# Value products moved behind the next pair's first score tiles, and the preparation of pairs moved further ahead

## The chip, the cores and the metric

The kernel runs on one core of a Trainium2 chip. The metric is the device time of one execution in microseconds, as the median of several runs. The core's engines run side by side, each through its own queue in order: TensorE (PE, with its weight loads PEld), VectorE (DVE), ScalarE (ACT), GpSimd (POOL) and SyncE (SP), whose queue issues all DMA transfers here.

## The reference

Sigmoid attention over 8 batches, 12 heads, 448 positions and 64 channels a head, followed by a feed-forward layer on 3584 tokens of width 768 with 2048 hidden units:

```python
scores = scale * np.matmul(q, k.transpose(0, 1, 3, 2)) - np.log(S)
attn = 1.0 / (1.0 + np.exp(-scores))
attn_out = np.matmul(attn, v)
x = attn_out.transpose(0, 2, 1, 3).reshape(B * S, H * D)
h = x @ w_in
g = np.where(h > 0.0, h, np.exp(np.minimum(h, 0.0)) - 1.0)
out = g @ w_out
```

Everything is float32 outside. Inside, after the first batch, each operand is split into a high and a low float16 part, and a product is made of three matmuls (high by high, low by high, high by low).

## The kernel before, in words

The work goes by batches `b` = 0 to 7 and, in a batch, by six pairs of heads `hp` = 0 to 5; `n = 6 b + hp` numbers the pairs. Batch 0 is computed in float32, while the two weight matrices are loaded, measured and split (`w_in_part`, `load_w_out`). From batch 1 on, TensorE, ScalarE, VectorE and SP keep the order in which the program is written (`manual_schedule`); GpSimd and all that comes earlier are ordered by a scheduler.

A pair is prepared in three steps, which `prepare_pair(n)` hands out one after the other. *Measure*: VectorE takes the largest magnitudes of the values (`mx<-rv`) and of queries and keys (`mt<-raw`), and spreads them on a diagonal (`dg`). *Scale* (`second`): TensorE sums the diagonal over the partitions (`pb`), VectorE reduces it (`al`, `pw`) and takes reciprocals, GpSimd makes the scales (`sc`). *Split* (`third`): ScalarE writes the high parts of queries, keys (`nat`) and values (`vn`), VectorE the low ones; SP issues the DMA that transposes `nat` into `qk`. The raw data lie in two buffers each (`raw`, and the two tiles `rvs` for values); the loads of a pair that comes two later follow the split in SP's queue, since that split empties their buffer.

A pair's own work is `scores(t)` for four tiles t (score tiles `psc` in PSUM, two buffers; the fourth tile is half as wide), `soften(t)` (sigmoid `sg` and scaled high part `at` on ScalarE, low part on VectorE), `values(t)` (value products, summed in `pav`), and `finish` (`xh`, the split result). At the end of a batch `hidden` rescales `xh` and calls `moe1`, which makes 16 tiles `ph` of 18 matmuls, whose exponentials and splits (`e`, `g`) ScalarE and VectorE do. The second product of the previous batch, `moe2`, is cut into steps of three matmuls each, 16 to a tile `po` of 48; `fill(n)` puts n such steps wherever TensorE would wait. An odd batch b has 96 steps (the product of an even batch has no tile of remaining rows), an even one 128. The PSUM tiles `po`, `pb` and most `ph` share three buffers (`pm`).

Before, a pair of a batch from 1 on runs on TensorE as: scores 0 and 1, five steps (eight in pair 0), scores 2 and 3, the rest of its share of steps, `pb`, its own four `values`. Between the first scores and the five steps the next pair is split and pair n + 3 is loaded; after the five steps pair n + 2 is measured, and behind the rest of the share it is scaled.

Of the kernel before, what the change touches and what calls it, by code (L numbers as in the profile page):

```python
# [9 lines left out]
F16 = mybir.dt.float16  # L10
BF16 = mybir.dt.bfloat16
F32 = mybir.dt.float32
# [20 lines left out]
def attention_ffn(  # L33
# [9 lines left out]
    nc = tc.nc  # L43
# [10 lines left out]
    HM = DM // NH  # L54
    SB, OB, AB = 4, 3, 3
    WF = 2
    WR, WT = 3, 2
    EXACT = 1
    SP = 4
    SKEW = 2  # L60
    W_IN = [1, 2, 3, 5, 6, 8, 8]
    W_LOAD = [1, 1]
# [236 lines left out]
    def prepare(b, hp, raw, rv, xs):  # L299
# [19 lines left out]
        def scales():  # L319
            product()  # L320
            sc = sb.tile([P, n + 3], F32, tag="sc", name=f"sc{u}", bufs=3)
            if b >= EXACT:
# [13 lines left out]
        def transposed(sc):  # L336
# [12 lines left out]
            for t, n_t, s in (  # L349
# [5 lines left out]
                )  # L355
            qk = sb.tile([P, 2, 2 * NC + 1, P], F16, tag="qk", name=f"qk{u}", bufs=2)
            nc.sync.dma_start_transpose(
# [3 lines left out]

            vn = sb.tile([P, 2, 2 * NC + 2, D], F16, tag="vn", name=f"vn{u}", bufs=2)
            split(vn[:, 0], vn[:, 1], rv, sc[:, 0:1])
# [4 lines left out]
    class Pair:  # L368


        def __init__(self, b, hp, x_scale, s_scale, qk, vs, xh, xs):
            self.b, self.hp, self.u = b, hp, f"{b}_{hp}"
            self.x_scale, self.s_scale = x_scale, s_scale
            self.qk, self.vs, self.xh, self.xs = qk, vs, xh, xs
            self.psc, self.sg, self.pav = {}, {}, None
# [46 lines left out]
        def values(self, g):  # L422
            if g == 0:
                self.pav = ps.tile([P, 512], F32, tag="pav", name=f"pav{self.u}")
            pav, sg, vv = self.pav, self.sg.pop(g), self.vs
            parts = [(0, 0), (1, 0), (0, 1)][: 2 * len(vv) - 1]
            for n, (i, k) in enumerate(parts):
                if g == NC:
                    nc.tensor.matmul(  # L429
                        pav[:, :S], vv[i][:, 2 * NC :].rearrange("p t d -> p (t d)"),  # L430
                        sg[k][:, 0], start=False, stop=(n == len(parts) - 1),
                    )
                    continue
                for j in range(2):
                    nc.tensor.matmul(  # L435
                        pav[rows[j], :S], vv[i][:, j * NC + g], sg[k][:, j],
                        start=(g == 0 and n == 0), stop=False,
                    )

        def finish(self):  # L440
            hp, xh = self.hp, self.xh
            split(xh[:, hp, 0], xh[:, hp, 1], self.pav[:, :S], self.x_scale)
            absmax(self.xs[:, 2, hp : hp + 1], xh[:, hp, 0])
# [37 lines left out]
    def moe1(b, g, xh, m, first, beside=None):  # L481
# [8 lines left out]
        for f in range(NF):  # L490

            if f == 3:
                ph = ps.tile([P, 512], F32, tag="pav", name=f"ph{b}_{f}")
            elif f == 8:
                ph = ps.tile([P, 2, 512], F32, tag="psc", name=f"ph{b}_{f}", bufs=2)[:, 0]
            else:
                ph = ps.tile([P, 512], F32, tag="pm", name=f"ph{b}_{f}", bufs=3)
# [100 lines left out]
    def prepare_pair(n):  # L598
# [4 lines left out]
        if hp == 0:  # L603
            xh_of[b] = sb.tile([P, NK, 2, S], F16, tag="xh", name=f"xh{b}", bufs=2)
            xs_of[b] = sb.tile([P, 3, NP], F32, tag="xs", name=f"xs{b}", bufs=2)
# [23 lines left out]
    def pair_of(n):  # L629
        b, hp = pairs[n]  # L630
        return Pair(b, hp, *ready.pop(n), xh_of[b], xs_of[b])

    def hidden(b, beside=None):

        xh, xs = xh_of.pop(b), xs_of.pop(b)
        whole = rescale(b, xh, xs)
# [24 lines left out]
    for n in range(EXACT * NP):  # L661
# [12 lines left out]
        for f in range(W_IN[n], W_IN[n + 1]):  # L674
            load_w_in(1)
            w_in_part(f)
    third = prepare_pair(EXACT * NP + 1)()
    load_pair(EXACT * NP + 2)
# [5 lines left out]


    E = mybir.EngineType
    with tc.manual_schedule(engines={E.PE, E.Activation, E.DVE, E.SP}):
        for b in range(EXACT, B):
# [4 lines left out]
            def fill(n):  # L693
                nonlocal left
                left -= n
                for _ in range(n):
                    next(tiles, None)

            for hp in range(NP):
                n = b * NP + hp  # L700
                share = left // (NP - hp)
                tail = 4 if hp == NP - 1 else 0
                p = pair_of(n)
                for t in range(2):
                    p.scores(t)
                    p.soften(t)
                third()
                if n + 3 < len(pairs):
                    loaded[n + 3] = load_qk(*pairs[n + 3]), load_v(*pairs[n + 3])

                gap = 8 if hp == 0 else 5
                fill(gap)
                second = prepare_pair(n + 2)
                for t in range(2, NC + 1):
                    p.scores(t)
                    p.soften(t)
                if b == EXACT and hp < NC:

                    step(3 if hp < NC - 1 else NF)
                if hp == NP - 1:  # L720
                    h = hidden(b)
                    next(h)
                fill(share - gap - tail)
                third = second()
                for t in range(NC + 1):
                    p.values(t)
                p.finish()
                fill(tail)
                if b == EXACT and hp == NC - 1:
                    out_scale(*of_moe2, slice(1, NH))  # L730
# [34 lines left out]
```

## Time and profile before

| | |
|---|---|
| median of 3 runs | 1274.88 us (1273.56 to 1275.74) |
| profiled execution | 1272.11 us, its span 1270.3 us |
| mean granted TensorE clock | 0.981 |
| TensorE busy | 1192.9 us, 94% of the span |
| VectorE busy | 841.5 us, 66% |
| ScalarE busy | 703.2 us, 55% |
| batch 0 and its weights, to the first output matmul | 170.83 us |
| attention of batch 1 | 100.66 us |
| attention of batches 2 / 3 / 7 | 96.42 / 87.70 / 84.88 us |
| first feed-forward product of a batch | 54.63 us |

"Attention of a batch" is the stretch from its first score tile (in batch 1, from the first output matmul) to the first matmul of `moe1`; it holds the steps of the previous batch's `moe2` as well. A row of the order-of-time view has start, length, engine, line, operation and tiles, and in brackets the idle time before it with what ended it. Where a length covers several instructions, the last one's tail is in it, so that durations are better read from start to start.

### The profile page before, as it was taken

How to read it: one execution, taken by the hardware profiler on the slowest of the kernel's cores; microseconds unless marked ns; L12 is line 12 of the kernel's file. 1: busy time of each engine (PE TensorE's matmuls, PEld its weight loads, DVE VectorE, ACT ScalarE, POOL GpSimd, SP SyncE). 2: the span in 40 equal slices, each digit the busy share in tenths (PEclk: the TensorE clock that was granted, in tenths of full speed). 3: DMA queues.
4: the chain of work that ended last, by engine and by line, in shares of the span. 5: the costliest groups of instructions: out<-in, count | busy, mean ns of one | idle time of the engine just before them, and what ended most of it. 6: DMA issues, size and time to landing. Idle time of an engine off the chain costs nothing.

```text
span 1270.3 us, 19231 instructions
## 1 busy us (share of the span) xinstructions
PE 1192.9 (94%) x7240; PEld 606.2 (48%) x7240; DVE 841.5 (66%) x1852; ACT 703.2 (55%) x1039; POOL 62.7 (5%) x269
## 2 busy tenths in 40 slices
PE   6779868999999998999999999999999999999998
PEld 2224434545455554445555554545455554455565
DVE  3787979875677657875677655885577756765500
ACT  5875878744666336754566436763566435673400
POOL 0000001000000000100000100000000000100000
PEclk8998989999999999999999999999999999999999
DMA  7836423420144203430144201440034401420000
GB/s 223 282 103 166 157 75 86 103 69 1 43 86 92 50 1 65 104 88 1 21 94 92 63 1 43 90 110 15 1 86 92 92 1 22 100 50 7 1 25 26
DMA packets 207133, 89.73 MB, mean 71 GB/s; under 512 B 177344, under 2 KB 196800, under 8 KB 207040
## 3 DMA queue, kind: packets, MB, share of 16 engines
q1 hardware_dynamic: 207040, 88.51, 28.1%
q8 instruction: 56, 0.92, 0.3%
q14 instruction: 37, 0.30, 0.1%
HBM read 58.20 MB, written 11.01 MB: 54 GB/s over the span
## 4 chain that ended last, share of the span: by engine, by line
PE 66%; DVE 12%; ACT 11%; DMA 5%; issue 5%; SPq 1%; POOL 0%; DVEq 0%; ACTq 0%
PE ph L501 30%; PE po L531 16%; PE pav L435 6%; PE po_r L531 5%; PE psc L385 5%; ACT sg L396 5%; DMA stage<-in_moe_w_in_dram 3%; PE pav L429 2%; ACT at L416 2%; DVE mt L126 2%; DVE nat L123 1%; DVE vn L123 1%; DMA wo<-in_moe_w_out_dram 1%; DVE mx L126 1%; DVE dg L106 1%
## 5 line engine op out<-in xcount | busy, mean ns | idle before, releaser
L501 PE MATMUL ph<-xh,wi 128*128 128x448 f16 x2304 | 443.0, 354 | 11.6 <-DVE xh L452 6.3
L531 PE MATMUL po<-wo,g 128*128 128x384 f16 x2304 | 392.8, 328 | 0.9 <-ACT wo L139 0.9
L531 PEld LDWEIGHTS <-g 128*128 128x128 f16 x2688 | 257.1, 98 | 197.5 <-issue 32.8
L501 PEld LDWEIGHTS <-wi 128*128 128x128 f16 x2304 | 225.4, 98 | 226.5 <-issue 13.4
L513 ACT ACTIVATE e<-ph,msc 128x448 f32<-128x448 f32 x128 | 80.8, 632 | 209.3 <-PE ph L501 209.3
L417 DVE SCALAR_TENSOR_TENSOR at<-sg,at 128x896 f16<-128x896 f32 x126 | 137.2, 1090 | 83.1 <-ACT at L416 82.9
L396 ACT ACTIVATE sg<-psc,bias,sc 128x896 f32<-128x896 f32 (+1 forms) x168 | 166.4, 990 | 1.7
L515 DVE TENSOR_SCALAR e<-e 128x448 f32<-128x448 f32 x128 | 50.4, 394 | 172.4 <-ACT e L513 172.4
L122 ACT ACTIVATE xh<-pav,sc 128x448 f16<-128x448 f32 x48 | 30.3, 632 | 183.5 <-PE pav L429 183.5
L385 PE MATMUL psc<-qk 64*128 64x448 f16 x1008 | 117.2, 355 | 12.3 <-ACT sg L396 12.3
L416 ACT ACTIVATE at<-sg 128x896 f16<-128x896 f32 x126 | 119.7, 950 | 4.2 <-DVE wo L158 0.2
L122 ACT ACTIVATE g<-e,msc 128x384 f16<-128x384 f32 (+1 forms) x192 | 96.1, 533 | 9.3 <-DVE e L516 8.3
L123 DVE SCALAR_TENSOR_TENSOR g<-e,msc,g 128x384 f16<-128x384 f32 (+1 forms) x192 | 94.6, 522 | 3.8 <-ACT g L122 3.4
L516 DVE SCALAR_TENSOR_TENSOR e<-ph,msc,e 128x448 f32<-128x448 f32 x128 | 87.5, 683 | 4.0
L435 PE MATMUL pav<-at,vn 128*64 128x448 f16 x756 | 82.9, 366 | 0.0
L385 PEld LDWEIGHTS <-qk 64*128 64x128 f16 x1008 | 41.8, 97 | 81.4 <-issue 57.5
L435 PEld LDWEIGHTS <-vn 128*64 128x64 f16 x756 | 40.2, 112 | 53.8 <-issue 32.4
L531 PE MATMUL po_r<-wo,g 128*128 128x384 f16 x384 | 64.7, 326 | 0.0
L123 DVE SCALAR_TENSOR_TENSOR nat<-raw,sc,nat 128x384 f16<-128x384 f32 (+1 forms) x126 | 59.1, 523 | 0.0
L122 ACT ACTIVATE nat<-raw,sc 128x384 f16<-128x384 f32 (+1 forms) x126 | 58.8, 529 | 0.0
L539 DVE TENSOR_SCALAR o<-po,osc 128x384 f32<-128x384 f32 x48 | 29.4, 613 | 40.5 <-PE po L531 35.8
L123 DVE SCALAR_TENSOR_TENSOR xh<-pav,sc,xh 128x448 f16<-128x448 f32 x48 | 32.6, 679 | 33.8 <-ACT xh L122 33.8
(104 smaller groups left out, 841.3 us busy)
## 6 DMA issues: line engine op xcount, KB each, us to landing
stage<-in_moe_w_in_dram SPq DMA_DIRECT2D x8, 1536.0 KB, 8.1
raw<-in_q_dram SPq DMA_DIRECT2D x96, 96.0 KB, 3.0
raw<-in_k_dram SPq DMA_DIRECT2D x96, 96.0 KB, 2.7
rv<-in_v_dram SPq DMA_DIRECT2D x48, 192.0 KB, 2.7
out_dram<-o SPq DMA_DIRECT2D x48, 192.0 KB, 2.1
wo<-in_moe_w_out_dram SPq DMA_DIRECT2D x19, 384.0 KB, 3.9
so<-in_moe_w_out_dram SPq DMA_DIRECT2D x13, 384.0 KB, 3.9
raw<-in_q_dram SPq DMA_DIRECT2D x48, 32.0 KB, 2.4
```

The costliest lines, as they stand in the source:

```text
L122: nc.scalar.mul(hi, src, s)
L123: nc.vector.scalar_tensor_tensor(lo, src, s, hi, op0=ALU.mult, op1=ALU.subtract)
L385: nc.tensor.matmul(psc[:, j, :S] if g < NC else psc[rows[j], 0, :S], kk[rows[j], o], qq[rows[j], :S], start=(n == 0), stop=(n == len(parts ...
L396: a = nc.scalar.activation(sg[:, :nb], psc[:, :nb, :S], AF.Sigmoid, bias=bias, scale=self.s_scale)
L416: nc.scalar.mul(hi, sg[:, :nb], 2.0**ATOP)
L417: nc.vector.scalar_tensor_tensor(lo, sg[:, :nb], 2.0**ATOP, hi, op0=ALU.mult, op1=ALU.subtract)
L435: nc.tensor.matmul(pav[rows[j], :S], vv[i][:, j * NC + g], sg[k][:, j], start=(g == 0 and n == 0), stop=False,)
L501: nc.tensor.matmul(ph[:, :S], wi[:, wj, c, f * P : (f + 1) * P], xh[:, c, xj], start=(n == 0), stop=(n == 3 * NK - 1),)
L513: a = nc.scalar.activation(e, ph[:, :S], AF.Exp, scale=inv)
L515: nc.vector.tensor_scalar(e, e, 1.0, -1.0, op0=ALU.min, op1=ALU.add)
L516: nc.vector.scalar_tensor_tensor(e, ph[:, :S], inv, e, op0=ALU.mult, op1=ALU.max)
L531: nc.tensor.matmul(po[:, :HM], lh(gj, f), wo[:, i, f, wj], start=(n == 0), stop=(n == 3 * NF - 1),)
```

## The change

Six things change together.

1. The four `values` of a pair no longer follow its own scores. They stand behind scores 0 and 1 of the next pair, and before that pair's scores 2 and 3; `finish` follows. The last pair of a batch keeps its own at the batch's end, and no steps are left behind them.
2. The steps of `moe2` are dealt out otherwise. Pair 0 has 24 between scores 1 and 2 and 12 between scores 2 and 3, and none after; pairs 1 to 4 have them all behind `pb` (12 in a batch of 96, 17 in one of 128); pair 5 has the rest.
3. The preparation is written as `scale_next`, `measure_next`, `split_next`, in this order behind a pair's fourth score tile, in pairs 0 to 4. The sixth set stands in the feed-forward stage, behind tiles 2, 4 and 5 (in batch 1 two sets). In a pair, what is scaled and split was measured in the pair before. Splits run two pairs ahead, from batch 2 on, and measuring three.
4. `qk` and `vn` have three buffers, `at` four, `sc` five, `xh` one (taken when its first pair finishes).
5. The last tile's value product is two matmuls of half the columns per part, where it was one of all columns.
6. In `moe1` the tiles 1, 4 and 9 lie in the score tiles' PSUM buffers, where only tile 8 did.

The core of the diff:

```diff
-    SB, OB, AB = 4, 3, 3
+    SB, OB, AB = 4, 3, 4
+    TAIL = 4
-            sc = sb.tile([P, n + 3], F32, tag="sc", name=f"sc{u}", bufs=3)
+            sc = sb.tile([P, n + 3], F32, tag="sc", name=f"sc{u}", bufs=5)
-            qk = sb.tile([P, 2, 2 * NC + 1, P], F16, tag="qk", name=f"qk{u}", bufs=2)
+            qk = sb.tile([P, 2, 2 * NC + 1, P], F16, tag="qk", name=f"qk{u}", bufs=3)
-            vn = sb.tile([P, 2, 2 * NC + 2, D], F16, tag="vn", name=f"vn{u}", bufs=2)
+            vn = sb.tile([P, 2, 2 * NC + 2, D], F16, tag="vn", name=f"vn{u}", bufs=3)
...
                 for j in range(2):
                     nc.tensor.matmul(
-                        pav[rows[j], :S], vv[i][:, j * NC + g], sg[k][:, j],
-                        start=(g == 0 and n == 0), stop=False,
+                        pav[rows[j], :S],
+                        vv[i][:, j * NC + g if g < NC else 2 * NC + j],
+                        sg[k][:, j if g < NC else 0],
+                        start=(g == 0 and n == 0),
+                        stop=(g == NC and n == len(parts) - 1),
                     )
...
-            elif f == 8:
+            elif f in (1, 4, 9):
                 ph = ps.tile([P, 2, 512], F32, tag="psc", name=f"ph{b}_{f}", bufs=2)[:, 0]
...
-    third = prepare_pair(EXACT * NP + 1)()
+    second = prepare_pair(EXACT * NP + 1)
...
+    at = EXACT * NP + 1
+    def scale_next():
+        nonlocal third
+        third = second()
+    def split_next():
+        nonlocal at
+        third()
+        load_pair(at + 2)
+        at += 1
+    def measure_next():
+        nonlocal second
+        second = prepare_pair(at + 1)
+    def ahead(n):
+        order = {}
+        for i in range(n):
+            order |= {6 * i + 2: scale_next, 6 * i + 4: measure_next, 6 * i + 5: split_next}
...
+            shares = [left // NP + d for d in (6, -4, -4, -4, -4, 10)]
+            prev = None
             for hp in range(NP):
                 n = b * NP + hp
-                share = left // (NP - hp)
-                tail = 4 if hp == NP - 1 else 0
+                last = hp == NP - 1
                 p = pair_of(n)
-                for t in range(2):
-                    p.scores(t)
-                    p.soften(t)
-                third()
-                if n + 3 < len(pairs):
-                    loaded[n + 3] = load_qk(*pairs[n + 3]), load_v(*pairs[n + 3])
-                gap = 8 if hp == 0 else 5
-                fill(gap)
-                second = prepare_pair(n + 2)
-                for t in range(2, NC + 1):
-                    p.scores(t)
-                    p.soften(t)
+                p.scores(0)
+                p.soften(0)
+                p.scores(1)
+                p.soften(1)
+                if prev:
+                    for t in range(NC + 1):
+                        prev.values(t)
+                else:
+                    fill(24)
+                p.scores(2)
+                if not prev:
+                    fill(12)
+                p.scores(NC)
+                if not last:
+                    scale_next()
+                if prev:
+                    prev.finish()
+                prev = p
+                p.soften(2)
+                p.soften(NC)
...
-                if hp == NP - 1:
-                    h = hidden(b)
-                    next(h)
-                fill(share - gap - tail)
-                third = second()
-                for t in range(NC + 1):
-                    p.values(t)
-                p.finish()
-                fill(tail)
+                if not last:
+                    measure_next()
+                    split_next()
+                    fill(shares[hp] - (36 if hp == 0 else 0))
+                else:
+                    h = hidden(b, ahead(2 if b == EXACT else 1))
+                    next(h)
+                    fill(left - TAIL)
+                    for t in range(NC + 1):
+                        p.values(t)
+                    p.finish()
+                    fill(left)
```

VectorE in pair 1 of batch 3, before. In the names, the digits behind the tile's own are batch and pair: `nat3_2` is pair 2 of batch 3; `at` and `sg` have the score tile's number ahead of them.

```order
L417 SCALAR_TENSOR_TENSOR at13_1_4711<-sg13_1_4709,at13_1_4711 128x896
L123 SCALAR_TENSOR_TENSOR nat3_2_4714<-raw3_2_3940,sc3_2_4656,nat3_2_4714 128x384
L123 SCALAR_TENSOR_TENSOR nat3_2_4714<-raw3_2_3940,sc3_2_4656,nat3_2_4714 128x128
L123 SCALAR_TENSOR_TENSOR nat3_2_4714<-raw3_2_3940,sc3_2_4656,nat3_2_4714 128x384
L123 SCALAR_TENSOR_TENSOR vn3_2_4723<-rv0_83,sc3_2_4656,vn3_2_4723 128x512
L126 TENSOR_REDUCE mx3_3_4752<-rv1_85 128x1
L126 TENSOR_REDUCE mt3_3_4754<-raw3_3_4553 128x7
L312 TENSOR_REDUCE mx3_3_4752<-mt3_3_4754 128x2
L315 TENSOR_TENSOR mx3_3_4752<-mx3_3_4752,mt3_3_4754 64x1 x2
L106 TENSOR_SCALAR dg_4760<-eye_81,mx3_3_4752 128x128 x3
L417 SCALAR_TENSOR_TENSOR at23_1_4773<-sg23_1_4771,at23_1_4773 128x896
```

The same engine and pair after the change:

```order
L418 SCALAR_TENSOR_TENSOR sg33_1_4892<-sg33_1_4892 128x448
L127 TENSOR_REDUCE mx3_4_4896<-rv0_83 128x1
L127 TENSOR_REDUCE mt3_4_4898<-raw3_4_4795 128x7
L313 TENSOR_REDUCE mx3_4_4896<-mt3_4_4898 128x2
L316 TENSOR_TENSOR mx3_4_4896<-mx3_4_4896,mt3_4_4898 64x1 x2
L107 TENSOR_SCALAR dg_4904<-eye_81,mx3_4_4896 128x128 x3
L124 SCALAR_TENSOR_TENSOR nat3_3_4908<-raw3_3_4331,sc3_3_4874,nat3_3_4908 128x384
L124 SCALAR_TENSOR_TENSOR nat3_3_4908<-raw3_3_4331,sc3_3_4874,nat3_3_4908 128x128
L124 SCALAR_TENSOR_TENSOR nat3_3_4908<-raw3_3_4331,sc3_3_4874,nat3_3_4908 128x384
L124 SCALAR_TENSOR_TENSOR vn3_3_4917<-rv1_85,sc3_3_4874,vn3_3_4917 128x512
L540 TENSOR_SCALAR o2_2_0_4966<-po2_2_0_4727,osc2_4588 128x384
L418 SCALAR_TENSOR_TENSOR at03_2_4978<-sg03_2_4976,at03_2_4978 128x896
```

Measuring stood behind the split and now stands ahead of it, and the whole set moved behind the fourth score tile. The pair measured, 3_4, is the one whose raw data the split of pair 0 (`nat3_2`) let SP load; the split behind it lets SP load the next.

ScalarE from pair 0's third sigmoid to pair 1's first in batch 3, before:

```order
L396 ACTIVATE sg23_0_4607<-psc23_0_4600,bias_64,sc3_0_3870 128x896
L416 ACTIVATE at23_0_4609<-sg23_0_4607 128x896
L396 ACTIVATE sg33_0_4619<-psc33_0_4612,bias_64,sc3_0_3870 128x448
L416 ACTIVATE sg33_0_4619<-sg33_0_4619 128x448
L122 ACTIVATE xh3_3772<-pav3_0_4665,sc3_0_3870 128x448
L396 ACTIVATE sg03_1_4697<-psc03_1_4690,bias_64,sc3_1_4057 128x896
```

And after:

```order
L397 ACTIVATE sg23_0_4762<-psc23_0_4693,bias_64,sc3_0_3832 128x896
L417 ACTIVATE at23_0_4764<-sg23_0_4762 128x896
L397 ACTIVATE sg33_0_4767<-psc33_0_4740,bias_64,sc3_0_3832 128x448
L417 ACTIVATE sg33_0_4767<-sg33_0_4767 128x448
L123 ACTIVATE nat3_2_4783<-raw3_2_3877,sc3_2_4753 128x384
L123 ACTIVATE nat3_2_4783<-raw3_2_3877,sc3_2_4753 128x128
L123 ACTIVATE nat3_2_4783<-raw3_2_3877,sc3_2_4753 128x384
L123 ACTIVATE vn3_2_4792<-rv0_83,sc3_2_4753 128x512
L397 ACTIVATE sg03_1_4812<-psc03_1_4805,bias_64,sc3_1_4225 128x896
```

The split (`nat`, `vn`) stood between the second and the third sigmoid of a pair; it now stands between one pair's last sigmoid and the next pair's first, and in pair 0 no steps of `moe2` are behind it on TensorE. SP's rows in a pair are the same as before: the transpose, six loads of queries and keys, three of values, and an output.

More of the change, by code (lines that the diff above doesn't have):

```diff
@@ L368, in attention_ffn, with __init__ @@
     class Pair:
-        def __init__(self, b, hp, x_scale, s_scale, qk, vs, xh, xs):
+        def __init__(self, b, hp, x_scale, s_scale, qk, vs, xs):
             self.b, self.hp, self.u = b, hp, f"{b}_{hp}"
             self.x_scale, self.s_scale = x_scale, s_scale
-            self.qk, self.vs, self.xh, self.xs = qk, vs, xh, xs
+            self.qk, self.vs, self.xs = qk, vs, xs
             self.psc, self.sg, self.pav = {}, {}, None
@@ L427, in values @@
             for n, (i, k) in enumerate(parts):
[L428 to L433, printed above, removed]
                 for j in range(2):
                     nc.tensor.matmul(
-                        pav[rows[j], :S], vv[i][:, j * NC + g], sg[k][:, j],
-                        start=(g == 0 and n == 0), stop=False,
+                        pav[rows[j], :S],
[3 more added lines that the diff above has]
+                        stop=(g == NC and n == len(parts) - 1),
                     )
         def finish(self):
-            hp, xh = self.hp, self.xh
+            b, hp = self.b, self.hp
+            if hp == 0:
+                xh_of[b] = sb.tile([P, NK, 2, S], F16, tag="xh", name=f"xh{b}")
+            xh = xh_of[b]
             split(xh[:, hp, 0], xh[:, hp, 1], self.pav[:, :S], self.x_scale)
@@ L603, in prepare_pair @@
         if hp == 0:
-            xh_of[b] = sb.tile([P, NK, 2, S], F16, tag="xh", name=f"xh{b}", bufs=2)
             xs_of[b] = sb.tile([P, 3, NP], F32, tag="xs", name=f"xs{b}", bufs=2)
@@ L630, in pair_of @@
         b, hp = pairs[n]
-        return Pair(b, hp, *ready.pop(n), xh_of[b], xs_of[b])
+        return Pair(b, hp, *ready.pop(n), xs_of[b])
     def hidden(b, beside=None):
-        xh, xs = xh_of.pop(b), xs_of.pop(b)
+        xh, xs = xh_of[b], xs_of[b]
         whole = rescale(b, xh, xs)
@@ L682, in attention_ffn, with beside @@
     of_moe2 = next(h)
+    at = EXACT * NP + 1
[14 more added lines that the diff above has]
+            order |= {6 * i + 2: scale_next, 6 * i + 4: measure_next, 6 * i + 5: split_next}
+        def beside(f):
+            order.get(f, int)()
+        return beside
+    third = None
     E = mybir.EngineType
```

## The prediction

> **What bounds the kernel now.** I read the page's line of TensorE first, then the busy time by stage, then who TensorE waits for, then one head pair in order of time. TensorE's line of the page, then the stage table; its columns are the stretch, its length, the busy time of TensorE, weight load, VectorE, ScalarE and GpSimd, the granted clock, and DMA.
>
> ```profile
> PE 1192.9 (94%) x7240; PEld 606.2 (48%) x7240; DVE 841.5 (66%) x1852; ACT 703.2 (55%) x1039; POOL 62.7 (5%) x269
> ```
> ```profile
> 170.83:271.49 100.66, 85.02 (x558) 42.19 (x559) 85.25 (x189) 73.13 (x105) 8.07 (x32) 0.93 0.39 90
> 326.13:422.55 96.42, 95.21 (x662) 50.04 (x661) 71.79 (x161) 61.46 (x84) 5.86 (x27) 1.00 0.38 85
> 422.55:477.18 54.63, 54.63 (x290) 28.14 (x289) 27.76 (x57) 18.67 (x30) 2.14 (x9) 1.00 0.03 9
> 477.18:564.88 87.70, 82.21 (x565) 41.07 (x565) 69.88 (x155) 61.09 (x82) 5.73 (x26) 0.98 0.40 89
> 1063.95:1148.83 84.88, 81.51 (x564) 40.81 (x563) 62.19 (x128) 59.17 (x78) 4.46 (x20) 0.98 0.29 64
> 491.77:495.18 3.41, 3.41 (x19) 1.26 (x15) 2.49 (x9) 0.00 (x0) 0.85 (x4) 0.50 0.58 126
> ```
>
> The first five stretches are the attention of batch 1, of batch 2, the first feed-forward product of batch 2, the attention of batch 3 and of batch 7. Attention stages of even batches hold 128 output steps of three matmuls ("long", 96.42 us), those of odd ones 96 ("short", 87.70 us). TensorE is busy through nearly all of them, but VectorE is busy 69.88 of 87.70 us: it is the next limit wherever a stage is squeezed. From 250 us on, TensorE's waits are these two alone, 19.1 us in all:
>
> ```profile
> PE pb L111 <- DVE dg L106: 12.4, 6, 2.1
> PE psc L385 <- ACT sg L396: 6.7, 6, 1.2
> ```
>
> The last row of the stage table shows what a wait can bring besides: right after one of 2.1 us the clock was 0.50 for 3.41 us.
>
> One pair of a short batch on TensorE, in order of time (start, length, work):
>
> ```profile
> 495.45 1.31 PE L385 MATMUL psc<-qk 64*128 64x448 f16 x12
> 496.69 2.61 PE L531 MATMUL po<-wo,g 128*128 128x384 f16 x15
> 499.24 1.43 PE L385 MATMUL psc<-qk 64*128 64x448 f16 x12
> 500.59 5.54 PE L531 MATMUL po<-wo,g 128*128 128x384 f16 x33
> 506.22 0.32 PE L111 MATMUL pb<-dg,ones 128*128 128x384 bf16 x1
> 506.47 1.89 PE L435 MATMUL pav<-at,vn 128*64 128x448 f16 x18
> 508.30 0.74 PE L429 MATMUL pav<-sg,vn 128*128 128x448 f16 x3
> 508.97 1.31 PE L385 MATMUL psc<-qk 64*128 64x448 f16 x12
> ```
>
> From start to start the pair takes 508.97-495.45 = 13.52 us: scores 1.24 and 1.35, value products 1.83 and 0.67, pb 0.25, 48 output matmuls 2.55 and 5.37 (about 0.163 each in the long run), and 0.26 in front of pb.
>
> **TensorE's work after the change.** Per pair: first scores after output matmuls 1.35; 24 half-width value matmuls 24/18 x 1.83 = 2.44 (six of them replace three full ones of 0.67 at 0.61, a gain of 0.06, nothing); second scores 1.3; together 5.1; pb 0.25. Pairs 1 to 4 then have 12 steps, 36 x 0.163 = 5.87 us, in a short batch and 17 steps, 8.31 us, in a long one. A short pair needs 11.2 us, a long one 13.65, where both had their share evenly before. Pair 0 holds 1.35 + 72 x 0.163 + 0.7 + 5.87 + 0.7 + 0.25 = 20.6 us and nothing after its pb. The old waits go: the second scores of pair 0 have 11.7 us of output matmuls ahead of them, and dg is made a pair earlier than pb uses it.
>
> **What is late next: ScalarE at pair 1.** ScalarE's queue around the split of the next pair, which now stands whole between pair 0's last sigmoid and pair 1's first:
>
> ```profile
> 526.36 0.95 ACT L416 ACTIVATE at<-sg 128x896 f16<-128x896 f32 x1
> 527.22 1.40 ACT L122 ACTIVATE nat<-raw,sc 128x384 f16<-128x384 f32 x3
> 528.53 0.71 ACT L122 ACTIVATE vn<-rv,sc 128x512 f16<-128x512 f32 x1
> 529.14 1.08 ACT L396 ACTIVATE sg<-psc,bias,sc 128x896 f32<-128x896 f32 x1
> ```
>
> Let E be the end of pair 0's last scores. Half a sigmoid and its scaling take about 1.3 us; the split waits for the scales, which VectorE makes from pb (1.4 us, rows below) and GpSimd finishes, to about E+2.2; it ends 1.92 later (527.22 to 529.14), at E+4.1. The sigmoids of pair 1 then end at E+5.2 and E+7.2 (1.1 and 0.86 a tile). TensorE has issued pb, two score tiles and the value products by E+4.05: it waits 1.15 and then 1.3, together 2.45 us, in each of the seven batches.
>
> **What is late next: the loads.** VectorE in one pair before, and the SP queue in two:
>
> ```profile
> 521.65 0.55 DVE L113 TENSOR_REDUCE al<-pb 128x3 f32<-128x384 f32 x1
> ...
> 522.90 0.16 DVE L290 RECIPROCAL xs<-xs 128x1 f32<-128x1 f32 x1
> ```
> ```profile
> 528.36 1.41 DVE L123 SCALAR_TENSOR_TENSOR nat<-raw,sc,nat 128x384 f16<-128x384 f32 x3
> 529.67 0.75 DVE L123 SCALAR_TENSOR_TENSOR vn<-rv,sc,vn 128x512 f16<-128x512 f32 x1
> 530.34 0.68 DVE L126 TENSOR_REDUCE mx<-rv 128x1 f32<-128x512 f32 x1
> 530.93 1.08 DVE L126 TENSOR_REDUCE mt<-raw 128x7 f32<-128x896 f32 x1
> ...
> 532.61 0.58 DVE L106 TENSOR_SCALAR dg<-eye,mx 128x128 bf16<-128x128 bf16 x3
> 533.11 1.08 DVE L417 SCALAR_TENSOR_TENSOR at<-sg,at 128x896 f16<-128x896 f32 x1
> 534.11 0.62 DVE L417 SCALAR_TENSOR_TENSOR sg<-sg 128x448 f16<-128x448 f32 x1
> ```
> ```profile
> 516.31 1.54 SPq L357 DMA_TRANSPOSE qk<-nat  x1
> ...
> 523.03 1.15 SPq L257 DMA_DIRECT2D rv<-in_v_dram  x2
> ...
> 529.83 1.56 SPq L357 DMA_TRANSPOSE qk<-nat  x1
> ...
> 537.24 1.15 SPq L257 DMA_DIRECT2D rv<-in_v_dram  x2
> ```
> ```profile
> rv<-in_v_dram SPq DMA_DIRECT2D x8, 16.0 KB, 2.3
> ```
>
> SP takes the transpose as soon as nat is done (529.77 to 529.83), then issues nine loads; the last starts 0.6 before the end of its row, at 523.6 and 537.8, and lands 2.3 later: 9.6 and 10.2 us after the transpose. I take 9.9. Before, VectorE split (nat, vn) and then measured (mx, mt, dg), so the values loaded behind one split were wanted 530.34-516.31 = 14.0 us later. After, it measures first and splits behind it, and what it measures is what the previous pair's split let load. That closes a loop: mx to dg's end 2.85 (530.34 to 533.19), nat 1.3 more, 0.1 of hand-overs, 9.9 until the values have landed: 14.15 us a round, against 11.2 us of TensorE work in a short pair and 13.65 in a long one. Behind the waiting mx stand, in VectorE's queue, dg (pb on TensorE waits for it, and all output matmuls behind pb), the split, and the next pair's at.
>
> A short batch, from its start: mx of pair 0 follows E by pb, al to xs (1.4), at and sg (1.6), so at 20.35+3.3 = 23.65; the next ones at 37.8, 51.95, 66.1 and 80.25. TensorE reaches pair 1's pb at 20.6+5.1+2.45 = 28.15, pair 2's at 28.15+11.2 = 39.35; dg is there at 37.8+2.85+0.05 = 40.7, a wait of 1.35. Pairs 3 and 4 are bound by the loop: pb at 54.85 and 69.0, waits of 2.95 each. After pair 4 VectorE still has measuring and splitting (4.9), two at (2.0), xh and its maximum (about 1.1, as two rows of the sg kind), at and sg (1.6), then the rescaling of xh, whose first product I put at 0.7 behind (between 0 and the 1.08 of an at): 80.25+10.3 = 90.55. There moe1 begins, +2.85 against 87.70. A long batch is bound by TensorE: 20.6 + 2.45 + 4 x 13.65 + last pair 5.1 + 11.74 + 2.44 = 96.95, +0.5; its pb of pair 4 comes due at 69.1, when dg is just there. The two waits at pair 1 stand within 3.3 us, and may cost a window at half clock, 1.7 us, at even odds: +0.85. (In a short batch that is hidden, for the loop is later.) Batch 7 loads only in its first two pairs: pair 3's pb at 54.85, then 0.25+5.87, 5.1+0.6+5.87, 5.1+5.87+2.44 to 85.95, +1.05.
>
> Batch 1 is the term that the trace bounds worst. 15.6 of its 100.66 us are idle, over w_out's last slices; 48 output matmuls more (7.8 us) now stand ahead of that wait, while the 12 pieces of w_out that ScalarE and VectorE scale at pair 0 now stand ahead of pair 1 with no cover. Its ends are the short batch's 90.55 (-10) and nothing of the idle saved with the loop on top (+5); I take -2. The feed-forward stage gains a pb of 0.25 in each of six batches, and 4.9 us of measuring and splitting on VectorE and 2.1 on ScalarE, covered by their idle half (27.76 and 18.67 busy of 54.63); two PSUM tiles more than before let TensorE run on: 1.5 us together. Everything up to 170 us changes only in order; I take 0, within 3 either way. New buffers of qk, vn, at and sc cost nothing by themselves.
>
> Sum: batches 3 and 5 2 x 2.85, long batches 3 x 1.35, batch 7 1.05, batch 1 -2, feed-forward 1.5: +10.3 us on the profiled execution's 1272.1 (span 1270.3 and 1.8 around it). The median of the runs is 2.8 above that execution, so 1274.9 + 10.3, rounded to 1285.
>
> A rule to weigh: the Trainium skill, "TensorE: Matmul & The Clock Gate" (Part 1), has the clock halved after an idle window of about 3.4 us. This trace has it halved after an idle 2.1 us, so the trace decides; by the rule none of the new waits would halve it, and the sum would be 2.5 us lower, 1282.5.
>
> **Rivals.**
> 1. Faster: the loop does not bind, because the values land in time or mx seldom waits. For it: before, the same loads had 4 us to spare. Then a short batch is 20.6+2.45+4 x 11.2+13.4 = 81.25 (-6.45, twice), batch 7 about 81.25 (-3.6), batch 1 -8, long and feed-forward as above: -19 us, 1256. It decides at a round of 13.4 us: 14 rounds bind in all (four in batches 1, 3, 5, two in 7), so 0.75 less a round cancels the sum. Against it: both bursts shown give 13.85 or more.
> 2. No change, within 0.2% (2.5 us, about what a measurement of this kernel can tell): rounds near 13.85, batch 1 at -6: 1277.
> 3. Slower by far: half-speed windows after each wait of 2.95 do land on the path, and VectorE's backlog reaches into moe1. Three windows of 1.7 in four batches: 1305.
> 4. The moved value products bring nothing of themselves: TensorE never waited for them before (no such row). That holds in my sum too; it is no separate time.
>
> **Chances.** My forecast's kind (slower, 1278 to 1299) 0.50; rival 3 0.11; rival 2 0.16; rival 1 0.14, and 0.09 for part of it, 1262 to 1272. Slower is 0.61, same 0.16, faster 0.23. The range 1260 to 1300 leaves out most of rivals 1 and 3; the likeliest case alone spans 1278 to 1299.
>
> **What would show it.** VectorE's mx waiting some 3 to 4 us for the DMA of rv, about 14 times; pb waiting for dg about ten times, 1.3 to 3 us; psc waiting for sg twice at pair 1 of every batch; stages of 90.5, 97 and 86 us. If mx does not wait, rival 1 holds and I am wrong; if the first feed-forward stage is over 56 us, the cover that I gave VectorE's work is not there.

## The result, and the profile after

The changed kernel takes 1327.47 us (median of four runs, 1326.48 to 1331.19), the kernel before 1274.94 beside it: a ratio of 1.0419 (1.0397 to 1.0441). I had forecast slower, by 10.3 us; it is 52.5. The profiled execution spans 1325.5 us where it spanned 1270.3, at a mean granted clock of 0.956 (0.981).

Busy time by stage of the changed kernel, columns as in the prediction's table: up to batch 1, attention of batch 1, the feed-forward stage of batch 1, attention of batch 2 (long), a feed-forward stage, attention of batch 3 and 5 (short) and 7, and one window within batch 2:

```profile
0.00:171.71 171.71, 137.07 (x616) 56.68 (x616) 127.78 (x265) 118.05 (x165) 7.79 (x34) 0.89 0.60 180
171.71:309.01 137.30, 89.65 (x577) 44.76 (x576) 84.56 (x181) 73.03 (x105) 9.62 (x31) 0.83 0.24 58
309.01:363.98 54.97, 54.97 (x294) 28.35 (x293) 40.25 (x104) 25.72 (x53) 3.42 (x13) 1.00 0.20 42
363.98:463.95 99.97, 97.06 (x679) 52.00 (x678) 66.00 (x144) 58.71 (x79) 7.26 (x28) 0.97 0.32 74
463.95:518.75 54.80, 54.80 (x292) 28.25 (x291) 32.88 (x73) 21.21 (x35) 1.95 (x7) 1.00 0.11 24
518.75:609.37 90.62, 82.24 (x582) 43.56 (x582) 62.27 (x135) 58.84 (x78) 6.75 (x26) 0.96 0.32 69
819.15:908.56 89.41, 80.63 (x582) 43.12 (x582) 62.27 (x135) 58.62 (x78) 6.75 (x26) 0.98 0.31 70
1118.92:1203.98 85.06, 78.69 (x582) 42.07 (x581) 56.36 (x115) 56.41 (x73) 5.50 (x20) 1.00 0.23 53
390.65:397.48 6.83, 6.07 (x24) 2.51 (x21) 6.66 (x15) 6.74 (x9) 1.12 (x5) 0.50 0.52 103
```

Beside the forecast, in us of the profiled execution (the other long batches took 99.94 and 100.52):

| stretch | forecast | measured |
|---|---|---|
| up to batch 1 | 0 | +0.9 |
| attention of batch 1 | -2 | +36.6 |
| long batches, three | +4.05 | +11.2 |
| short batches, two | +5.7 | +4.6 |
| batch 7 | +1.05 | +0.2 |
| seven feed-forward stages | +1.5 | +1.7 |
| sum | +10.3 | +55.2 |

Two thirds of the loss stand in one stretch of 137 us. TensorE's idle part of that stretch (length less busy time) went from 15.64 to 47.65 us, and its busy time grew by 4.63. Who TensorE waits for there (first row), and from 310 us to the end (the two largest there; each row has the waiter, whom it waits for, total us, times, longest):

```profile
PE psc L386 <- DMA qk<-nat: 46.7, 5, 18.3
```
```profile
PE psc L386 <- ACT sg L397: 21.4, 15, 2.1
PE pb L112 <- DVE dg L107: 8.8, 6, 2.7
```

The wait for `qk`, the transposed queries and keys, did not exist in the kernel before. One round of batch 1, on TensorE (a pair from its first scores to the next pair's), then VectorE, then SP's transposition, and the time from issue to landing over the five of this stage:

```profile
253.54 2.42 PE L386 MATMUL psc<-qk 64*128 64x448 f16 x12 [7.17 <-DMA qk<-nat]
...
260.44 0.34 PE L112 MATMUL pb<-dg,ones 128*128 128x384 bf16 x1
260.61 6.01 PE L532 MATMUL po<-wo,g 128*128 128x384 f16 x36
273.12 2.42 PE L386 MATMUL psc<-qk 64*128 64x448 f16 x12 [6.50 <-DMA qk<-nat]
```
```profile
260.81 0.56 DVE L114 TENSOR_REDUCE al<-pb 128x3 f32<-128x384 f32 x1 [0.75 <-PE pb L112]
...
264.79 0.68 DVE L127 TENSOR_REDUCE mx<-rv 128x1 f32<-128x512 f32 x1
...
267.55 1.40 DVE L124 SCALAR_TENSOR_TENSOR nat<-raw,sc,nat 128x384 f16<-128x384 f32 x3
```
```profile
269.02 1.56 SPq L358 DMA_TRANSPOSE qk<-nat  x1
```
```profile
DMA to landing us min/median/max: 4.0/4.0/4.2
```

Read as a chain: scores to pb 6.9 us, pb to the measuring 4.35 (its reduction, xh, at, sg stand ahead), measuring 2.76, the low half of the split 1.4, transposition 4.1: 273.12 - 253.54 = 19.6 us a round, with 13 us of work for TensorE in it. In batch 1 the set behind pair hp splits pair hp + 1, the very next one. From batch 2 on it splits pair hp + 2, and the same chain has a whole pair more. Here mx waits for nothing: the load loop of the prediction is not what binds. In the four waits of 6 to 8 us the granted clock falls to a half late in the wait, for 6.83 us (271.19 to 278.01 us in the round shown), so that the first scores take 2.42 us instead of 1.31.

### The profile page after: what moved, and what is told of

Its sections match the earlier page's. It is cut to its first block, busy times and chain, and to the rows that moved or that the text cites. A ratio compares the mean times of both kernels' runs of the same rounds, so it can differ in the third digit from the quotient of the medians.

```text
span 1325.5 us, 19447 instructions
## 1 busy us (share of the span) xinstructions
PE 1206.0 (91%) x7378; PEld 621.6 (47%) x7378; DVE 840.3 (63%) x1852; ACT 701.8 (53%) x1039; POOL 71.2 (5%) x269
## 4 chain that ended last, share of the span: by engine, by line
PE 69%; DVE 15%; DMA 6%; ACT 5%; SPq 3%; issue 2%; DVEq 0%; ACTq 0%
PE ph L502 29%; PE po L532 21%; PE psc L386 6%; PE pav L430 6%; PE po_r L532 5%; DVE at L418 2%; DMA qk<-nat 2%; DMA rv<-in_v_dram 2%; DVE nat L124 1%; ACT sg L397 1%; DVE mt L127 1%; DMA stage<-in_moe_w_in_dram 1%; DMA wo<-in_moe_w_out_dram 1%; SPq L258 1%; SPq L268 1%
## 5 line engine op out<-in xcount | busy, mean ns | idle before, releaser
L532 PEld LDWEIGHTS <-g 128*128 128x128 f16 x2688 | 264.7, 99 | 194.0 <-issue 26.2
L386 PE MATMUL psc<-qk 64*128 64x448 f16 x1008 | 125.8, 373 | 68.4 <-DMA qk<-nat 46.7
L124 DVE SCALAR_TENSOR_TENSOR g<-e,msc,g 128x384 f16<-128x384 f32 (+1 forms) x192 | 94.5, 521 | 0.7 <-ACT g L123 0.2
L430 PEld LDWEIGHTS <-vn 128*64 128x64 f16 x1008 | 56.4, 114 | 53.4 <-issue 24.0
L127 DVE TENSOR_REDUCE mx<-rv 128x1 f32<-128x512 f32 x48 | 32.7, 682 | 65.2 <-DMA rv<-in_v_dram 65.2
```

The source lines that it names most:

```text
L124: nc.vector.scalar_tensor_tensor(lo, src, s, hi, op0=ALU.mult, op1=ALU.subtract)
L386: nc.tensor.matmul(psc[:, j, :S] if g < NC else psc[rows[j], 0, :S], kk[rows[j], o], qq[rows[j], :S], start=(n == 0), stop=(n == len(parts ...
L430: nc.tensor.matmul(pav[rows[j], :S], vv[i][:, j * NC + g if g < NC else 2 * NC + j], sg[k][:, j if g < NC else 0], start=(g == 0 and n == ...
L532: nc.tensor.matmul(po[:, :HM], lh(gj, f), wo[:, i, f, wj], start=(n == 0), stop=(n == 3 * NF - 1),)
```

## Experiments

All ratios are to the kernel before, run beside them on the same chip. Stage rows have the columns of the tables above.

**1. Batch 1 in the old order.** Batch 1 gets its own copy of the old loop body, and its pair 1 is scaled ahead of the batch again, as before the change (that line is not shown); batches 2 to 7 are unchanged.

```diff
...
+            if b == EXACT:
+                for hp in range(NP):
+                    n = b * NP + hp
+                    share = left // (NP - hp)
...
+                    third()
+                    load_pair(n + 3)
+                    gap = 8 if hp == 0 else 5
+                    fill(gap)
+                    second = prepare_pair(n + 2)
...
+                continue
```

> Batch 1 alone is written in the order of the kernel before (split between the first and the third score tile, own value products at the pair's end, even shares of steps); batches 2 to 7 stay as changed. Theory A (in batch 1 a pair is split only one pair ahead, so that the way from its split over the transposition to its first scores lies on TensorE's path): batch 1's attention goes from 137.3 us back to about 100.7, the time to 1327.5 - 36.6 = 1291 us. Rival B (batch 1 is long because its w_out pieces have lost their cover) expects the same here, since that cover comes back too. Rival C (the length of batch 1 comes from what the scheduler did with the work ahead of it): the attention of batch 1 stays above 120, the time above 1310.

Measured: 1289.61 us, 1.0134 (1.0097 to 1.0171). The row is batch 1's attention:

```profile
166.80:270.97 104.17, 88.31 (x578) 44.08 (x577) 91.09 (x202) 76.50 (x113) 8.93 (x37) 0.90 0.38 88
```

It takes 104.17 us, 3.5 above the row before, but began 4 us earlier and ends where it used to end (270.97 against 271.49). So the loss is made inside batch 1, by the order there, and not ahead of it: C falls. A and B stay.

**2. Batch 1 two pairs ahead.** The order of batch 1 stays as changed, but the pair that pair 0 would split (pair 1) is split already in batch 0's stage, and pair 2 is measured there.

```diff
-    second = prepare_pair(EXACT * NP + 1)
+    third = prepare_pair(EXACT * NP + 1)()
     load_pair(EXACT * NP + 2)
+    third()
+    load_pair(EXACT * NP + 3)
+    second = prepare_pair(EXACT * NP + 2)
-    at = EXACT * NP + 1
+    at = EXACT * NP + 2
-                    h = hidden(b, ahead(2 if b == EXACT else 1))
+                    h = hidden(b, ahead(1))
```

> As the changed kernel, but pair 1 of batch 1 is split, and pair 2 measured, already during the first feed-forward product of batch 0, so that batch 1 too splits two pairs ahead; its feed-forward stage then has one set of preparation where it had two. The w_out pieces stay where they are. Theory A (one pair ahead is the reason): the five waits of psc for qk go; pb of pair 1 follows ScalarE's w_out pieces and split, about 10 us earlier than now; then rounds of about 14.2 us of the load loop where there are now about 20; batch 1's attention about 101 us where it was 137.3, the time 1291 us (up to 3 more if the early set costs something). Rival B (w_out pieces without cover): only the start of pair 1 can move, the four rounds behind it stay near 20 us, batch 1 above 125 us, the time 1317 or more.

Measured: 1297.83 us, 1.0190 (1.0163 to 1.0218). Attention of batch 1, then SP's queue, first of this kernel, then of the changed one at the same place:

```profile
185.33:278.45 93.12, 81.63 (x577) 43.59 (x576) 76.96 (x167) 68.09 (x98) 9.22 (x32) 0.96 0.33 76
```
```profile
124.35 1.56 SPq L358 DMA_TRANSPOSE qk<-nat  x1
...
132.25 1.54 SPq L232 DMA_DIRECT2D wo<-in_moe_w_out_dram  x3
```
```profile
124.30 3.50 SPq L232 DMA_DIRECT2D wo<-in_moe_w_out_dram  x7
```

The attention fell from 137.30 to 93.12 us with w_out's pieces where they were: A holds. B, which kept the four rounds behind pair 1's first scores near 20 us, falls as the main cause: from first scores to first scores the last three take 11.1, 12.4 and 13.8 us, where the changed kernel's take 20.0, 19.6 and 19.9. The first still takes 19.2, with a wait of 3.66 us for ScalarE in pair 1, so the pieces of w_out keep a part of their own. The stage is even below my 101; part of that may be the later start, by which w_out's slices are further along. The time missed the 1291 because the stage began at 185.33 instead of 171.71: the additional set's transposition and nine loads stand in SP's queue ahead of w_out's next slices, which start 8 us later. Whether that is all of the 13.6 us is not shown.

**3. Split ahead of measuring.**

```diff
-                    measure_next()
                     split_next()
+                    measure_next()
-        second = prepare_pair(at + 1)
+        second = prepare_pair(at)
-            order |= {6 * i + 2: scale_next, 6 * i + 4: measure_next, 6 * i + 5: split_next}
+            order |= {6 * i + 2: scale_next, 6 * i + 4: split_next, 6 * i + 5: measure_next}
```

> As the changed kernel, but in each set of preparation the split stands ahead of the measuring, so that a split never waits behind the loads of the pair that is measured next. Nothing else moves. Theory A for batch 1 (split to scores on the path): each of its five rounds loses the 2.85 us of measuring, about -14 us. The load loop of the prediction (measuring waits for values that the split before it let load): it is gone, mx no longer waits for rv, pb no longer for dg; batches 3 and 5 go from 90.6 and 89.4 to about 83, batch 7 from 85.1 to about 82, long batches stay near 100: -17 us. Both together 1296 us. If the loop was not what bound the short batches (rival: VectorE's own work did), only batch 1 gains: 1313. If rival B holds for batch 1 and the loop is real: 1310.

Measured: 1294.28 us, 1.0169 (1.0143 to 1.0194). Attention of batches 1, 2, 3, 5 and 7, then the only wait of TensorE from 310 us on:

```profile
170.55:293.52 122.97, 88.29 (x578) 44.42 (x576) 84.70 (x181) 72.81 (x106) 9.62 (x31) 0.86 0.27 65
348.48:447.69 99.21, 95.84 (x678) 51.62 (x678) 66.40 (x144) 58.71 (x79) 7.63 (x28) 0.98 0.32 74
502.49:586.03 83.54, 80.17 (x582) 42.23 (x582) 64.30 (x140) 58.34 (x77) 7.12 (x26) 0.98 0.37 84
795.57:879.18 83.61, 80.23 (x583) 42.22 (x582) 64.32 (x140) 58.34 (x77) 7.12 (x26) 0.98 0.36 83
1088.91:1172.36 83.45, 80.07 (x582) 42.22 (x581) 56.65 (x115) 56.41 (x73) 5.86 (x20) 0.98 0.23 54
```
```profile
PE psc L386 <- ACT sg L397: 19.5, 12, 2.2
```

Every number is within 2 us of the expectation: batch 1 loses 14.3, the short batches 7.1 and 5.8, batch 7 1.6, the long one shown 0.8, and pb waits for dg no more. So both the load loop and the chain through the split are real, and they lie in different batches: the loop binds the short ones, the chain binds batch 1.

**4. Cover at pair 1, first try.** Pair 0's steps between its scores go from 24 and 12 to 20 and 10; the remaining six were to stand behind pb, by the old formula.

```diff
-                    fill(24)
+                    fill(20)
-                    fill(12)
+                    fill(10)
-                    fill(shares[hp] - (36 if hp == 0 else 0))
+                    fill(shares[hp] - (30 if hp == 0 else 0))
```

> As the changed kernel, but six of pair 0's 36 steps stand behind its pb (20 and 10 stay between its scores), so that TensorE has 2.9 us of output matmuls while ScalarE splits between pair 0's last sigmoid and pair 1's first. Prediction's term (ScalarE late at pair 1): the two waits of psc for sg there (2.15 and 0.76 us) and the half-clock window behind them (6.8 us long in the long batches) go: each long batch about -5 us, 100 to 95; in short batches only what the load loop does not take back, 0 to -1.5 each. Together about -17 us, 1310. If these waits come from something else than ScalarE's queue, or the half-clock window from something else than the waits: within 3 us of 1327.5.

Measured: 1324.26 us, 1.0401 (1.0375 to 1.0427). The edit did not do what its expectation says: the share of pair 0 is 22 or 27, the count behind pb -8 or -3, and the steps went to the last pair. TensorE in batch 2 shows no po between pb and the next scores:

```profile
382.04 0.34 PE L112 MATMUL pb<-dg,ones 128*128 128x384 bf16 x1
382.31 1.36 PE L386 MATMUL psc<-qk 64*128 64x448 f16 x12
...
388.21 1.04 PE L386 MATMUL psc<-qk 64*128 64x448 f16 x6 [2.14 <-ACT sg L397]
```

It says only that steps taken out from between pair 0's scores neither cause nor cure the waits.

**5. Cover at pair 1, with the six steps behind pb.**

```diff
-                    fill(shares[hp] - (36 if hp == 0 else 0))
+                    if hp == 0:
+                        left -= shares[hp] - 36
+                        for _ in range(6):
+                            next(tiles, None)
+                    else:
+                        fill(shares[hp])
```

(beside the 20 and 10 of the try before)

> As the changed kernel, but pair 0's 36 steps are dealt out 20, 10 and 6, the 6 of them really behind its pb (in the run before this one, the count there came out negative and no step was issued). Prediction's term (ScalarE late at pair 1, where TensorE has no steps behind pair 0's pb): the waits of psc for sg at pair 1 (2.15 and 0.76 us) go in every batch from 2 on, and the half-clock window behind them. Long batches 100 to about 94.5 (20.6 + 4 x 13.65 + 19.3). In short ones pair 0's pb, and with it the load loop, is 2.9 us earlier: 90.6 and 89.4 to 87.7 and 86.5, batch 7 85.1 to 82.2. Batch 1 stays. Together -25 us: 1302. If the wait only moves to another place of ScalarE's queue, half of it: 1315. If ScalarE's split is not the reason: 1325 or more.

Measured: 1298.67 us, 1.0197 (1.0172 to 1.0223). Batches 2, 3, 5 and 7:

```profile
360.39:455.03 94.64, 94.07 (x678) 50.93 (x678) 65.48 (x144) 58.97 (x79) 7.31 (x28) 1.00 0.36 79
509.84:597.23 87.39, 81.79 (x582) 43.43 (x582) 62.10 (x135) 58.75 (x78) 6.80 (x26) 0.96 0.34 72
801.98:889.05 87.07, 80.56 (x582) 43.05 (x582) 62.11 (x135) 58.64 (x78) 6.79 (x26) 0.98 0.33 72
1093.55:1177.06 83.51, 79.94 (x581) 42.22 (x581) 56.29 (x115) 56.54 (x73) 5.52 (x20) 0.98 0.23 54
```

ScalarE is late at pair 1, as forecast, and work for TensorE there covers it: 2.9 us of it bring a long batch 5.33 us. That the split is what makes ScalarE late is read from the order of its queue; the split was not moved by itself. The idle part of a row (length less TensorE's busy time) fell from 2.91 to 0.57, which is 2.34; the other 3.0 were the half clock, now 1.00 in this row.

**6. One more set in pair 0 of batch 1.**

```diff
+                if b == EXACT and hp == 0:
+                    scale_next()
+                    measure_next()
+                    split_next()
                 if prev:
...
-                    h = hidden(b, ahead(2 if b == EXACT else 1))
+                    h = hidden(b, ahead(1))
```

> As the changed kernel, but batch 1 has one more set of preparation in its pair 0, right behind scores 1 and ahead of the 24 steps (pair 1 is split there, pair 2 measured), so that it splits two pairs ahead from pair 0's end on; its feed-forward stage has one set instead of two. Nothing stands ahead of w_out's loads, as it did in the run that prepared the pair in batch 0's stage (there batch 1's attention took 93 us, but began at 185 instead of 172). Theory A: attention of batch 1 from 137.3 to 93 to 98 us (the set's 4.9 us on VectorE may lie in the way of w_out's pieces), its begin unchanged near 171.7: 1283 to 1288. Rival D (the later begin is the price of the second set, wherever it stands): 1297.

Measured: 1297.85 us, 1.0194 (1.0170 to 1.0218). The start was kept, at 170.28 us, so the later begin that rival D spoke of did not come; but attention took 109.79 us, not 93 to 98, and the expectation missed. The time is D's 1297 all the same: the stage ends at 280.07 us, where experiment 2's ended at 278.45, so the set cost about as much in either place. The first rows of TensorE show where part of it goes:

```profile
171.82 0.32 PE L112 MATMUL pb<-dg,ones 128*128 128x384 bf16 x1 [1.20 <-DVE e L517]
176.40 6.54 PE L532 MATMUL po<-wo,g 128*128 128x384 f16 x31 [4.26 <-DVE e L517]
```

The set's pb took the PSUM buffer that the first output tile would have had, and that tile waited for a tile of the feed-forward stage to be read. I had counted the set's VectorE time and not its buffer.

**7. The value products alone, in the kernel before.**

```diff
+                if hp:
+                    for t in range(NC + 1):
+                        prev.values(t)
+                    prev.finish()
+                prev = p
                 third()
...
-                for t in range(NC + 1):
-                    p.values(t)
-                p.finish()
+                if hp == NP - 1:
+                    for t in range(NC + 1):
+                        p.values(t)
+                    p.finish()
```

> The kernel before, with one part of the change: a pair's value products (and its finish) stand behind scores 0 and 1 of the next pair, ahead of that pair's split; the last pair of a batch keeps its own. at has four buffers, xh one. Shares of steps, preparation, qk and vn stay as before. Rival 4 of the prediction (the moved products bring nothing of themselves, since TensorE never waited for them): 1274.9, within 2.5. The other theory: they put 3.1 us of TensorE work between the first scores and pb, and so cover VectorE's measuring: the six waits of pb for dg in the last pairs (2.1 each, 12.4) and the half-clock windows behind three of them go, up to -17 us, 1258; pair 0's waits of psc for sg (6.7 us) stay, since pair 0 has no moved products.

Measured: 1265.37 us, 0.9932 (0.9909 to 0.9955): between the two expectations. Batches 2 and 3, and in batch 3 the start of two pairs and the last pb:

```profile
326.85:422.94 96.09, 94.74 (x662) 50.45 (x661) 72.56 (x163) 60.91 (x84) 7.65 (x31) 1.00 0.40 87
477.57:562.98 85.41, 81.10 (x565) 41.55 (x565) 69.64 (x155) 60.75 (x82) 9.14 (x26) 0.98 0.41 92
```
```profile
507.00 1.31 PE L385 MATMUL psc<-qk 64*128 64x448 f16 x12
...
520.16 1.31 PE L385 MATMUL psc<-qk 64*128 64x448 f16 x12
...
558.37 0.32 PE L111 MATMUL pb<-dg,ones 128*128 128x384 bf16 x1 [0.76 <-DVE dg L106]
```

A short pair takes 13.16 us instead of 13.52 (the 0.26 in front of pb is gone), and the last pb of the batch waits 0.76 instead of 2.03. Rival 4 was wrong: moving the products does bring something, 2.3 us in batch 3; that fits the products that now stand ahead of the last pb, which take 2.4 us at full clock (my 3.1 was too much). Pair 0's wait of 2.1 stays, having no moved products. A new wait comes with the order, of psc for qk in pair 1 (0.43 us in batch 3, 2.0 in all): TensorE gets to the next pair's scores sooner, and the way over the transposition shows here too.

**8 and 9. The repairs together.** Number 8 is 3, 5 and 6 in one (in the additional set too the split comes first). Number 9 moves its additional set:

```diff
                 else:
                     fill(20)
+                if b == EXACT and hp == 0:
+                    scale_next()
+                    split_next()
+                    measure_next()
                 p.scores(2)
```

> The changed kernel with three repairs together: one more set in pair 0 of batch 1 (two pairs ahead there too), the split ahead of the measuring in every set, and six of pair 0's steps behind its pb. If the three causes are apart from each other: batch 1's attention about 93, long batches 94.5, short ones and batch 7 about 79 (20.6 + 4 x 11.2 + 13.4), the feed-forward stages 54.9: 171 + 93 + 283.5 + 237 + 384 + 67 and 1.8 around it, 1238 us, a ratio of 0.971 to the kernel before. If VectorE's own work (some 70 us a batch) bounds the short batches once the waits are gone, they stay at 83: 1250.

> As the kernel with three repairs, but the additional set in pair 0 of batch 1 stands behind the first 20 steps instead of ahead of them. In the run before, its pb came ahead of the first output tile and took one of the three PSUM buffers that they share, and the first output matmuls waited 4.3 us. If that wait was the price of the set: batch 1's attention 101.7 to about 97, the time 1244 to 1240 us. If ScalarE's and VectorE's work in pair 0 (w_out's pieces and two splits) sets the end of batch 1's first pairs, the wait for sg at pair 1 (4.9 us there) grows by what the start gains: 1244, within 2.

Measured: 1244.12 us, 0.9775 (0.9744 to 0.9807), and 1237.67 us, 0.9714 (0.9698 to 0.9730). Number 8 missed its 1238 by 6 us, in batch 1, which took 101.62 us and not 93. Number 9, attention of batches 1, 2, 3 and 7:

```profile
166.10:263.27 97.17, 85.25 (x578) 43.50 (x577) 88.37 (x198) 74.08 (x110) 10.95 (x37) 0.91 0.40 92
318.08:412.73 94.65, 94.08 (x679) 50.94 (x678) 66.18 (x144) 58.83 (x79) 7.67 (x28) 1.00 0.34 77
467.53:546.75 79.22, 78.57 (x582) 41.66 (x581) 64.00 (x140) 58.80 (x77) 7.16 (x26) 1.00 0.38 86
1034.50:1113.57 79.07, 78.41 (x581) 41.57 (x581) 56.36 (x115) 56.77 (x73) 5.88 (x20) 1.00 0.24 57
```

From batch 2 on the repairs add up as expected (94.5 and 79): TensorE is busy through all but about 0.6 us of each stage, and VectorE, with 64 of 79 us, does not bind. The version is 37 us below the kernel before and 90 below the changed one. The place of the set, with the PSUM buffer that its pb took, was the price in number 8: batch 1 goes from 101.62 to 97.17 us, and the wait of 4.26 is gone, with a wait for sg longer by 0.85 (5.75 where it was 4.90).

## Why the prediction was wrong, step by step

- **Batch 1 is the step that failed.** I gave it -2, with ends of -10 and +5; it was +36.6, two thirds of the whole loss. Both ends were taken from the short batch's working, which has the split two pairs ahead. That this holds only from batch 2 on stood in my own description of the change. Had I walked through pair 0 and pair 1 of batch 1 as I did for batch 3, the rows at hand gave the chain: pb to the split from VectorE's rows, 2.85 of measuring, 1.4 of splitting, and a transposition that before was issued 6.2 us ahead of its use (516.31, and the pair's scores at 522.48) and now comes directly ahead of it, its 4.1 us on the path. I spoke of idle time over w_out. Its pieces did lengthen the chain, but only at its start: from pb to the measuring took 10.43 us in the first round, 6.19 in the second and 4.35 in the one shown above, some 8 us more together than at that last pace.

```profile
193.17 0.34 PE L112 MATMUL pb<-dg,ones 128*128 128x384 bf16 x1
```
```profile
203.60 0.68 DVE L127 TENSOR_REDUCE mx<-rv 128x1 f32<-128x512 f32 x1
```

- **The half-speed window was mis-sized.** I put it at 1.7 us at even odds, 0.85 a long batch, from windows of 3.41 us; it was 6.83 us long in each of the three and cost 3.0 in batch 2 (experiment 5). With it the long batches come to 100 instead of 97.8. The waits themselves were right: 2.15 and 0.76 at pair 1 in batch 2, 2.91 where I had 2.45, by the mechanism I named. Without batch 1 the forecast was +12.3 and the measurement is +18.6 us, so the sign was no luck; most of that difference is half clock.
- **The load loop was right.** mx waits for the DMA of rv, 22 times and 53.7 us together (I had 14 times, 3 to 4 us each; the long batches wait too, hidden). Batch 3's five transpositions start at 546.58 and the last at 602.90, four rounds of 14.08 us on average; I had 14.15:

```profile
DVE mx L127 <- DMA rv<-in_v_dram: 53.7, 22, 3.6
```
```profile
546.58 1.56 SPq L358 DMA_TRANSPOSE qk<-nat  x1
...
602.90 1.57 SPq L358 DMA_TRANSPOSE qk<-nat  x1
```

  The short batches took 90.62 and 89.41 (90.55 forecast), batch 7 85.06 (85.95). pb waited for dg six times and not ten. Three of my ten were batch 1's, where the longer chain binds and no such wait stands; batches 3, 5 and 7 have two each (I had 3, 3 and 1). The first of batch 3's three is missing because TensorE came to pair 2's pb 41.93 us into the stage (560.68), and not at my 39.35; the longer wait and the half clock at pair 1 fit this, but it was not tested. Without the loop the short batches are at 83.5 (experiment 3).
- **The feed-forward stages were right**: +1.7 for 1.5, the first one 54.97, below the 56 that I had named as the sign of missing cover, with VectorE at 40.25 busy in it.
- **The rivals.** 1 (faster) and 2 fell with the loop. 3 (slower by far) had the right sign, but of its half-clock windows behind the loop's waits only one came (574.97 to 578.39 us, in batch 3); the costly ones stand at pair 1 of the long batches and in batch 1, and VectorE's backlog did not reach into the feed-forward stage. 4 fell in experiment 7. None had the chain through the transposition in batch 1.
- **The clock.** The Trainium skill, "TensorE: Matmul & The Clock Gate" (Part 1), asks for an idle window of about 3.4 us; here 2.15 us and 0.76 behind it were enough in batch 2 (window row above), so by its rule the sum would have been still further off.

Left open: the stretch ahead of batch 1 ended between 166.1 and 171.7 us in kernels that hardly differ there (171.71 in the changed one, 166.80 in experiment 1, 166.10 in number 9). I have no cause for that; of the 37 us gained over the kernel before, up to 4.7 (170.83 - 166.10) are of this kind.

## What to carry to other kernels

When preparation moves further ahead, ask for each stage how far ahead it really is: the first stage still runs at the old depth, and a reorder that takes its cover away there shows up in no steady stage. Follow the chain of a unit (scale, split, transfer, use) through that stage row by row instead of bounding it by the steady one. In an in-order queue, put what frees a buffer (the split) ahead of what waits for the next load (the measuring), and count the PSUM buffer of a moved step along with its time.

## What the hardware showed that I had not expected

The same waits cost very different amounts of half clock. The waits at pair 1 (2.15 us, then 0.7 to 1.2) were followed by 6.83 us at 0.50 in batches 2, 4 and 6, by 3.41 in batches 3 and 5, and by none in batch 7, in one execution. The traces show what decides. All half-clock stretches of a trace begin on one grid of 3.413 us (from 271.19 to 390.65 us are 35 steps), and what counts is how long TensorE is idle within one window of that grid. Two windows of batch 2, then two of batch 7, in the columns of the tables above:

```profile
387.24:390.65 3.41, 1.26 (x14) 0.66 (x12) 3.28 (x10) 3.28 (x6) 0.87 (x3) 1.00 0.00 0
390.65:394.06 3.41, 2.65 (x14) 0.87 (x11) 3.37 (x6) 3.38 (x5) 0.00 (x0) 0.50 0.33 63
...
1141.58:1145.00 3.42, 1.73 (x20) 0.89 (x15) 3.29 (x9) 2.71 (x5) 1.45 (x4) 1.00 0.01 2
1145.00:1148.41 3.41, 1.73 (x14) 0.81 (x14) 3.38 (x9) 3.35 (x5) 0.00 (x0) 1.00 0.13 26
```

In batch 2 the 2.15 us lie whole in the first window (3.41 less 1.26 busy), so the next is at half clock; that one holds the 0.76, so the one behind it is at half clock too, and being full it ends the stretch. In batch 7 the grid cuts the same waits into 1.69 and 1.68, and nothing is halved. Over all 3237 such windows of the eleven traces (the two kernels and the nine experiments), from 205 us to 72 us before the end: a window at full clock was followed by half clock each time when TensorE was idle for 2.02 us of it or more, never below 1.79, and either way between; a window at half clock was followed by full clock each time with 0.56 us idle or less, and by half clock again from 0.66 on. The Trainium skill, "TensorE: Matmul & The Clock Gate" (Part 1), has the window free-running at 3413 ns; the grid agrees with it, though here 2.02 us idle in it was enough. So the price of a wait depends on where in the grid it falls. No run set that position on purpose; the rule is read from the traces as they fell.
